# A linear-attention block with a gated feed-forward on one core: first tiles centred only, no self-waits on TensorE, half chunks joined, denominators sent through DRAM, folded weight in ten products

## The chip, the cores and the metric

The kernel runs on one core of a Trainium2 chip. The metric is the device time of one execution in microseconds (us). Executions of one kernel on the same chip are compared by the ratio of the means of their fast runs, with a 95% interval. A profile is one execution taken with the hardware profiler, and its span (first to last instruction) is 1.7 to 1.9 us shorter than the time of the same execution. A few executions of the kernel before lay over 1.5% above its fastest; they count as slow and are left out of the ratios.

## The reference, cut to what matters

```python
# x [1, 2048, 640], wqkv [640, 1920], wo [640, 640], w1 [640, 1728], w2 [1728, 640]; bf16; 32 heads of 20
xn  = layernorm(x)                              # no weight, no bias
q, k, v = split_heads(xn @ wqkv)
pq, pk  = phi(q), phi(k)                        # phi(t) = (t + 1 if t > 0 else exp(t)) + 1e-6
kv  = einsum("bhsd,bhse->bhde", pk, v)          # 20 x 20 per head
z   = einsum("bhsd->bhd", pk)
den = einsum("bhqd,bhd->bhq", pq, z) + 1e-6
s   = merge_heads(einsum("bhqd,bhde->bhqe", pq, kv) / den) @ wo
g   = silu(relu(xn @ w1) @ w2)
out = x + s * g
```

## The kernel before

Tokens are cut into 16 tiles of 128 (T) and four chunks of 512 (J); the model dimension into five blocks of 128 (C). The feed-forward width is 13 chunks of 128 and one half chunk of 64 rows. The kernel never forms V: it builds G = xn^T pk, and from it the small per-head matrices kv, and multiplies those with wo into one 640 x 640 weight for the query features (the folded weight). The order on TensorE is:

1. the opening: dummy matmuls that warm the clock, transposes, and the K products of the first four tiles;
2. the first-weight stage: Q and hidden (H) blocks of five matmuls 128x512, with the K tiles of the next chunk between them; near its end the denominators (den);
3. G: five blocks of 32 matmuls;
4. the second-weight stage and S: hidden times w2, its half chunks, the kv and folded-weight products in between, and per token tile an S product of ten matmuls, which VectorE multiplies by the gate and adds to x.

A small scheduler follows which engine last wrote and read each buffer, and puts the waits in. These are the parts that the change and the argument touch.

```python
# the scheduler: has engine E already seen `agent`?
return vc.get(agent[0], 0) >= agent[1] + 1
...
# loads, all on the SP queue: four x tiles, all of the K weights, all of the Q weights, then the rest
for t in range(4):
    x_load(t)
w_load(wqk[:, :, D:2 * D], A_wqkv[:, D:2 * D], ("wk",))
w_load(wqk[:, :, 0:D], A_wqkv[:, 0:D], ("wq",))
...
def LN_stats(t):          # VectorE: bn_stats twice, bn_aggr; GpSimd: + eps, then ** -0.5 -> rsy
    ...
def LN_norm(t):           # VectorE: (x - mean) * rsy
    last_norm[0] = sc.op("DVE", lambda eng: eng.tensor_scalar(
        out=xn[:, t, :], in0=xin[:, t % XR, :], scalar1=mv[:, t, 0:1], scalar2=rsy[:, t:t + 1],
        op0=ALU.subtract, op1=ALU.mult), R=[("xin", t % XR), ("mv", t), ("rsy", t)], W=[("xn", t)])
...
def z_add():              # GpSimd: adds one tile's pk to the running sum z
    t = zpend.pop(0)
    sc.op("POOL", lambda eng: eng.tensor_tensor(out=zacc[:, :], in0=zacc[:, :], in1=pk[:, t, :], op=ALU.add),
          R=[("zacc",), ("pk", t)], W=[("zacc",)])
...
# second weight: issued on SP as soon as the last H group has been read
for a in range(2):
    c0, c1 = (0, 7) if a == 0 else (7, NF)
    dma("SP", lambda eng, c0=c0, c1=c1: eng.dma_start(
        w2_sb[:, c0:c1, :], B_w2[P * c0:P * c1, :].rearrange("(c p) n -> p c n", p=P)),
        W=[("w2", a)], extra=[lastW1])
...
def expand(m):            # spreads 1/den from 32 heads over 128 features with four matmuls into PSUM
    fns = [(lambda eng, i=i: eng.matmul(ps[4 + i], lhsT=EmQ[H * i:H * (i + 1), m, :], rhs=rden[H * i:H * (i + 1), :],
                                        start=True, stop=True)) for i in range(J)]
    ...                   # and VectorE multiplies the query features by it
for k in range(C):
    lastG = G_block(k, gb[k % 2])
    expand(k)
...
def U(p, hook=None):      # two token tiles times w2: 26 matmuls, 26 more, then four half-chunk matmuls
    ...
```

Of the kernel before, what the change touches and what calls it, by code (L numbers as in the profile page):

```python
# [20 lines left out]
class Sched:  # L21
# [19 lines left out]
    def _known(self, E, agent):  # L41
        vc = self.vc[E]
        if agent[0] == "D":
            return vc.get(agent, False)
        return vc.get(agent[0], 0) >= agent[1] + 1
# [58 lines left out]
    def _update_res(self, agent, R, W):  # L104
# [8 lines left out]
        for key in W:  # L113
            st = self.res.get(key)
            if st is None:
                st = self.res[key] = _Res()
            else:
                assert st.w is None or st.nread > 0 or key in Rset or key in self.allow_unread, (
                    "unread overwrite of %r by %r (prev writer %r)" % (key, agent, st.w))
            st.w = agent  # L120
            st.r = {}
            st.nread = 0
# [89 lines left out]
def bass_recurrent_scan__linear_attn_block__dense_activation_relu__prompt_kernel(  # L212
# [23 lines left out]
    XR = 8  # L236

# [3 lines left out]
    h_lo = [(P * c) // DH for c in range(C)]  # L241
    h_hi = [-(-(P * (c + 1)) // DH) for c in range(C)]

    def cs_of_m(m):
        return [c for c in range(C) if DH * h_lo[c] < P * (m + 1) and DH * h_hi[c] > P * m]

    bf = dt.bfloat16
    f32 = dt.float32

# [12 lines left out]
    kvp = reg3[:, 0:C * D].rearrange("p (c n) -> p c n", c=C)  # L262
    outb = reg3[:, C * D:(C + NOUT) * D].rearrange("p (a n) -> p a n", a=NOUT)
    tmpo = reg3[:, (C + NOUT) * D:(C + 2 * NOUT) * D].rearrange("p (a n) -> p a n", a=NOUT)
# [18 lines left out]
    wo_sb = reg7[:, 0:C * D].rearrange("p (c n) -> p c n", c=C)  # L283
# [3 lines left out]
    ek = nc.alloc_sbuf_tensor("ek", [P, NEK, 2, D], bf)  # L287
    er = nc.alloc_sbuf_tensor("er", [P, NER, 2, 512], bf)
    ident = nc.alloc_sbuf_tensor("ident", [P, P], bf)
    EmQ = nc.alloc_sbuf_tensor("EmQ", [P, C, P], bf)  # L290
    mh = nc.alloc_sbuf_tensor("mh", [P, C, H], f32)
    zmat = nc.alloc_sbuf_tensor("zmat", [P, C, H], bf)
    zacc = nc.alloc_sbuf_tensor("zacc", [P, D], f32)
    zhl = nc.alloc_sbuf_tensor("zhl", [P, 2, D], bf)
    ones = nc.alloc_sbuf_tensor("ones", [P, 1], bf)
    mhalf = nc.alloc_sbuf_tensor("mhalf", [P, 1], f32)
    denS = nc.alloc_sbuf_tensor("denS", [P, 512], f32)
    rden = nc.alloc_sbuf_tensor("rden", [P, 512], bf)
    stats = nc.alloc_sbuf_tensor("stats", [P, T, 2, 6], f32)
    mv = nc.alloc_sbuf_tensor("mv", [P, T, 2], f32)  # L300
    rsv = nc.alloc_sbuf_tensor("rsv", [P, T], f32)
    rsy = nc.alloc_sbuf_tensor("rsy", [P, T], f32)

# [7 lines left out]
    NDS = 90  # L311
# [15 lines left out]

    def x_load(t):
        sl = t % XR
        dma("SP", lambda eng: eng.dma_start(xin[:, sl, :], x2[tok(t), :]), W=[("xin", sl)])  # L330

    def w_load(dst, src, key, extra=()):
        dma("SP", lambda eng: eng.dma_start(dst, src.rearrange("(c p) n -> p c n", p=P)), W=[key], extra=extra)

    for t in range(4):
        x_load(t)
    w_load(wqk[:, :, D:2 * D], A_wqkv[:, D:2 * D], ("wk",))
    w_load(wqk[:, :, 0:D], A_wqkv[:, 0:D], ("wq",))
    for t in range(4, XR):
        x_load(t)  # L340
    F1 = 7 * P
    w_load(w1_sb[:, :, 0:F1], B_w1[:, 0:F1], ("w1", 0))
    w_load(w1_sb[:, :, F1:FF], B_w1[:, F1:FF], ("w1", 1))


    sc.op("POOL", lambda eng: eng.memset(ident[:], 0.0), W=[("ident",)])
# [6 lines left out]
    NWARM = 42  # L353
    sc.group("PE", [(lambda eng: eng.matmul(ps[7][:, 0:P], lhsT=ident[:], rhs=ident[:], start=True, stop=True))
                    for _ in range(NWARM)], R=[("ident",)], W=[("ps", 7)])
    sc.allow_unread.add(("ps", 7))

    def build_consts():
        em = EmQ[0:H, :, :].rearrange("p c n -> p (c n)")
        sc.op("POOL", lambda eng: eng.memset(em, 1.0), W=[("Em",)])  # L360
        sc.op("POOL", lambda eng: eng.affine_select(out=em, in_=em, compare_op=ALU.is_ge, fill=0.0,
                                                    base=0, pattern=[[1, D]], channel_multiplier=-DH),
              R=[("Em",)], W=[("Em",)])
        sc.op("POOL", lambda eng: eng.affine_select(out=em, in_=em, compare_op=ALU.is_ge, fill=0.0,
                                                    base=DH - 1, pattern=[[-1, D]], channel_multiplier=DH),
              R=[("Em",)], W=[("Em",)])
        for qd in range(1, 4):
            dma("SP", lambda eng, qd=qd: eng.dma_start(EmQ[H * qd:H * (qd + 1), :, :], EmQ[0:H, :, :]),
                R=[("Em",)], W=[("Em4", qd)])
# [6 lines left out]
              R=[("mh",)], W=[("mh",)])  # L376


    def LN_stats(t):
        xv = xin[:, t % XR, :]  # L380
        for a in range(2):
            sc.op("DVE", lambda eng, a=a: eng.bn_stats(stats[:, t, a, :], xv[:, HN * a:HN * (a + 1)]),  # L382
                  R=[("xin", t % XR)], W=[("stats", t, a)])
# [5 lines left out]
                                                    op=ALU.pow), R=[("rsv", t), ("mhalf",)], W=[("rsy", t)])  # L389

# [8 lines left out]

    def transposes(t, b):  # L400
        psb = ps[b].bitcast(bf)
        sc.group("PE", [(lambda eng, c=c: eng.transpose(psb[:, P * c:P * (c + 1)], xn[:, t, P * c:P * (c + 1)], ident[:]))
                        for c in range(C)], R=[("xn", t), ("ident",)], W=[("ps", b)])

    def xnT_copy(t, b):
        psb = ps[b].bitcast(bf)
        sc.op("ACT", lambda eng: eng.activation(out=xnT[:, :, tok(t)],
                                                in_=psb[:, 0:C * P].rearrange("p (c q) -> p c q", c=C),
                                                func=ACTF.Copy), R=[("ps", b)], W=[("xnT", t)])
# [5 lines left out]
    def K_mm(t, b, halves=(0, 1)):  # L415
        fns = []
        for a in halves:
            for k in range(C):
                fns.append(lambda eng, a=a, k=k: eng.matmul(  # L419
                    ps[b + a][:, 0:HN], lhsT=xnT[:, k, tok(t)], rhs=wqk[:, k, D + HN * a:D + HN * (a + 1)],  # L420
                    start=(k == 0), stop=(k == C - 1)))
        sc.group("PE", fns, R=[("xnT", t), ("wk",)], W=[("ps", b + a) for a in halves])
# [7 lines left out]

    def K_exp(t, b):
        e_ = ek[:, t % NEK, 0, :]
        sc.op("ACT", lambda eng: eng.activation(out=e_.rearrange("p (a n) -> p a n", a=2), in_=ps2(b, HN), func=ACTF.Exp),  # L433
              R=[("ps", b), ("ps", b + 1)], W=[("ek_e", t % NEK)])

    def K_relu(t, b):
        r_ = ek[:, t % NEK, 1, :]
        sc.op("ACT", lambda eng: eng.activation(out=r_.rearrange("p (a n) -> p a n", a=2), in_=ps2(b, HN), func=ACTF.Relu),
              R=[("ps", b), ("ps", b + 1)], W=[("ek_r", t % NEK)])
# [11 lines left out]
    def K_ev(t, b):  # L451
        K_exp(t, b)
        K_relu(t, b)
        K_fin(t)

# [3 lines left out]
    def nextb():  # L459
        b = RB[ring[0] % len(RB)]  # L460
        ring[0] += 1
        return b

    qi = [0]

    def Q_block(j, f):
# [9 lines left out]
        if j == 0:  # L476
            sc.op("ACT", lambda eng: eng.activation(out=r_, in_=ps[b], func=ACTF.Relu), R=[("ps", b)], W=[("er_r", es)])
# [311 lines left out]
    for m in range(C):  # L789
        W_block(m)  # L790
# [39 lines left out]
```

## Time and profile before

| | before |
|---|---|
| time, median of 4 runs | 234.38 us (232.65 to 235.73) |
| span of the profile, mean clock | 233.1 us, 0.992 |
| first K matmul / end of the first four K tiles | 9.36 / 17.71 us |
| end of the first-weight stage (E) | 116.37 us |
| end of G | 140.2 us |
| last S matmul | 229.3 us |

(The prediction was made when three of the four runs were known, with a median of 233.63.)

To read a profile of such a kernel, one takes the busy shares and the slices first; they say which engine never rests. Here that is TensorE, so the rest of the time goes into the chain of work that ended last, read in order of time. The prediction below does this. Two more lines of the page of before are needed later. One is the group of the normalisations on VectorE (busy time, mean ns of one, then the engine's idle time before them), the other the memory traffic of the whole run.

### The profile page before, as it was taken

How to read it: one execution, taken by the hardware profiler on the slowest of the kernel's cores; microseconds unless marked ns; L12 is line 12 of the kernel's file. 1: busy time of each engine (PE TensorE's matmuls, PEld its weight loads, DVE VectorE, ACT ScalarE, POOL GpSimd, SP SyncE). 2: the span in 40 equal slices, each digit the busy share in tenths (PEclk: the TensorE clock that was granted, in tenths of full speed). 3: DMA queues.
4: the chain of work that ended last, by engine and by line, in shares of the span. 5: the costliest groups of instructions: out<-in, count | busy, mean ns of one | idle time of the engine just before them, and what ended most of it. 6: DMA issues, size and time to landing. Idle time of an engine off the chain costs nothing.

```text
span 233.1 us, 3514 instructions
## 1 busy us (share of the span) xinstructions
PE 223.4 (96%) x1461; PEld 134.7 (58%) x1471; DVE 104.8 (45%) x199; ACT 86.9 (37%) x141; POOL 47.5 (20%) x67
## 2 busy tenths in 40 slices
PE   7599999999999999999999999999999999999993
PEld 7464555544544555444466667666666667666662
DVE  4588941595527951681526446111230404041335
ACT  2289676655675666654521113322020202202020
POOL 4335923317623154420000004000000000000001
PEclk9979999999999999999999999999999999999999
DMA  5999620011400123000088007500101001010103
GB/s 166 376 399 182 138 106 3 0 30 42 61 6 0 28 59 28 0 0 3 0 272 265 0 0 262 191 0 3 58 0 59 28 28 59 0 56 3 56 0 113
DMA packets 20879, 17.95 MB, mean 77 GB/s; under 512 B 8864, under 2 KB 20864, under 8 KB 20864
## 3 DMA queue, kind: packets, MB, share of 16 engines
q1 hardware_dynamic: 20864, 17.74, 26.3%
q8 instruction: 11, 0.18, 0.3%
q14 instruction: 4, 0.03, 0.0%
HBM read 13.03 MB, written 2.62 MB: 67 GB/s over the span
## 4 chain that ended last, share of the span: by engine, by line
PE 87%; DVE 6%; DMA 4%; issue 1%; SPq 1%; ACT 0%; DVEq 0%
PE psT L715 25%; PE psT L491 21%; PE psT L665 10%; PE psT L419 9%; PE psT L743 9%; PE psT L468 7%; DMA reg<-in_A_wqkv_dram 3%; DVE pqT L485 2%; PE psT L692 2%; PE psT L725 1%; DVE er L483 1%; DMA reg<-reg 1%; PE psT L504 1%; SPq L330 1%; DVE stats L382 1%
## 5 line engine op out<-in xcount | busy, mean ns | idle before, releaser
L715 PE MATMUL psT<-reg,hT 128*128 128x320 bf16 x416 | 59.2, 299 | 0.4
L491 PE MATMUL psT<-reg 128*128 128x512 bf16 x252 | 56.8, 379 | 0.5 <-issue 0.2
L715 PEld LDWEIGHTS psT<-reg,hT 128*128 128x128 bf16 x416 | 40.0, 98 | 18.1 <-PE psT L715 2.7
L491 PEld LDWEIGHTS psT<-reg 128*128 128x128 bf16 x260 | 25.3, 98 | 29.2 <-issue 0.4
L495 ACT ACTIVATE hT<-psT 128x512 bf16<-128x512 f32 x52 | 31.1, 598 | 19.6 <-PE psT L491 19.5
L757 DVE TENSOR_TENSOR reg<-psT,reg 128x640 bf16<-128x640 f32 (+1 forms) x17 | 13.3, 784 | 55.6 <-PE psT L743 55.6
L732 ACT ACTIVATE reg<-psT 128x640 bf16<-128x640 f32 x16 | 10.4, 700 | 69.6 <-PE psT L725 69.6
L419 PE MATMUL psT<-reg 128*128 128x320 bf16 x160 | 25.8, 309 | 3.1 <-DMA reg<-in_A_wqkv_dram 2.6
L428 POOL TENSOR_TENSOR zacc<-zacc,reg 128x640 f32<-128x640 f32 x16 | 22.6, 1410 | 27.4 <-DVE reg L447 27.2
L743 PE MATMUL psT<-reg,pqT 128*128 128x320 bf16 x160 | 22.9, 299 | 0.0
L419 PEld LDWEIGHTS psT<-reg 128*128 128x128 bf16 x160 | 15.8, 101 | 11.9 <-issue 2.8
L665 PE MATMUL psT<-reg 128*128 128x320 bf16 x160 | 22.6, 299 | 0.0
L468 PE MATMUL psT<-reg 128*128 128x512 bf16 x98 | 21.8, 379 | 0.2 <-issue 0.2
L657 DVE TENSOR_TENSOR pqT<-pqT,psT 128x512 bf16<-128x512 bf16 x20 | 12.4, 682 | 16.6 <-PE psT L653 16.6
L743 PEld LDWEIGHTS psT<-reg,pqT 128*128 128x128 bf16 x160 | 15.1, 98 | 7.4 <-issue 1.9
L665 PEld LDWEIGHTS psT<-reg 128*128 128x128 bf16 x160 | 15.2, 98 | 7.0 <-issue 1.3
L760 POOL TENSOR_TENSOR reg<-reg 128x320 bf16<-128x320 bf16 x1 | 0.8, 789 | 87.0 <-DVE reg L757 87.0
L382 DVE BATCH_NORM_STATS2 stats<-reg 128x6 f32<-128x320 bf16 x32 | 14.0, 479 | 5.5 <-DMA reg<-in_A_x_dram 5.5
L468 PEld LDWEIGHTS psT<-reg 128*128 128x128 bf16 x100 | 9.7, 98 | 11.5 <-issue 0.4
L433 ACT ACTIVATE ek<-psT 128x640 bf16<-128x640 f32 x16 | 11.3, 704 | 10.6 <-PE psT L419 10.4
L445 DVE TENSOR_SCALAR ek<-ek 128x640 bf16<-128x640 bf16 x16 | 5.1, 320 | 21.6 <-ACT ek L433 21.4
L475 ACT ACTIVATE er<-psT 128x512 bf16<-128x512 f32 x20 | 12.0, 599 | 7.5 <-PE psT L468 4.7
(59 smaller groups left out, 151.8 us busy)
## 6 DMA issues: line engine op xcount, KB each, us to landing
reg<-in_A_x_dram SPq DMA_DIRECT2D x16, 160.0 KB, 6.6
reg<-in_A_x_dram SPq DMA_DIRECT2D x4, 640.0 KB, 6.9
out_dram<-reg SPq DMA_DIRECT2D x15, 160.0 KB, 1.8
reg<-in_B_w_dram SPq DMA_DIRECT2D x2, 1120.0 KB, 7.6
reg<-in_A_wqkv_dram SPq DMA_DIRECT2D x2, 800.0 KB, 7.4
reg<-in_B_w_dram SPq DMA_DIRECT2D x1, 1040.0 KB, 12.2
reg<-in_B_w_dram SPq DMA_DIRECT2D x1, 960.0 KB, 8.4
wv_sb<-in_A_wqkv_dram SPq DMA_DIRECT2D x1, 800.0 KB, 5.1
```

What stands on the lines that cost most here:

```text
L382: sc.op("DVE", lambda eng, a=a: eng.bn_stats(stats[:, t, a, :], xv[:, HN * a:HN * (a + 1)]), R=[("xin", t % XR)], W=[("stats", t, a)])
L419: fns.append(lambda eng, a=a, k=k: eng.matmul(ps[b + a][:, 0:HN], lhsT=xnT[:, k, tok(t)], rhs=wqk[:, k, D + HN * a:D + HN * (a + 1)], star ...
L428: sc.op("POOL", lambda eng: eng.tensor_tensor(out=zacc[:, :], in0=zacc[:, :], in1=pk[:, t, :], op=ALU.add), R=[("zacc",), ("pk", t)], W=[( ...
L468: sc.group("PE", [(lambda eng, k=k: eng.matmul(ps[b], lhsT=wqk[:, k, P * f:P * (f + 1)], rhs=xnT[:, k, schunk(j)], start=(k == 0), stop=(k ...
L475: sc.op("ACT", lambda eng: eng.activation(out=e_, in_=ps[b], func=ACTF.Exp), R=[("ps", b)], W=[("er_e", es)])
L491: a = sc.group("PE", [(lambda eng, k=k: eng.matmul(ps[b], lhsT=w1_sb[:, k, P * f:P * (f + 1)], rhs=xnT[:, k, schunk(j)], start=(k == 0), s ...
L495: sc.op("ACT", lambda eng: eng.activation(out=hT[:, f, schunk(j)], in_=ps[b], func=ACTF.Relu), R=[("ps", b)], W=[("hT", j, f)])
L657: sc.op("DVE", lambda eng, i=i: eng.tensor_tensor(out=pqT[:, m, schunk(i)], in0=pqT[:, m, schunk(i)], in1=ps[4 + i], op=ALU.mult), R=[("ps ...
L665: fns.append(lambda eng, t=t, a=a: eng.matmul(ps[b + a][:, 0:HN], lhsT=xn[:, t, P * k:P * (k + 1)], rhs=pk[:, t, HN * a:HN * (a + 1)], sta ...
L715: fns.append(lambda eng, u=u, t=t, f=f, n=n: eng.matmul(ps[bs[n] + u][:, 0:HN], lhsT=hT[:, f, tok(t)], rhs=w2_sb[:, f, HN * n:HN * (n + 1) ...
L743: sc.group("PE", [(lambda eng, c=c, a=a: eng.matmul(ps[b + a][:, 0:HN], lhsT=pqT[:, c, tok(t)], rhs=wf[:, c, HN * a:HN * (a + 1)], start=( ...
L757: sc.op("DVE", lambda eng: eng.tensor_tensor(out=tmpo[:, os_, lo:hi].rearrange(shp, a=na), in0=src, in1=g_sb[:, t, lo:hi].rearrange(shp, a ...
```

## The change

The intent is to take TensorE's hiccups away. The K products of the first four tiles run on x minus its mean, and the factor 1/sigma comes in later as a scale on ScalarE. TensorE no longer waits for its own earlier groups. The half chunks of two pairs are done in one group of eight. The spreading of 1/den leaves TensorE: the reciprocals are written to DRAM twenty-fold and read back in the layout that VectorE needs. The kv matrix is cut into six blocks of whole heads instead of five of 128 rows, so that each block of the folded weight needs two contractions instead of two or three: ten passes, 20 matmuls, where 26 were. Q blocks and S products are spread between other work. The diff cut to its core:

```diff
@@ scheduler @@
+        if E == "PE" and agent[0] == "PE":
+            return True
@@ loads @@
-    for t in range(4):
-        x_load(t)
-    w_load(wqk[:, :, D:2 * D], A_wqkv[:, D:2 * D], ("wk",))
-    w_load(wqk[:, :, 0:D], A_wqkv[:, 0:D], ("wq",))
+    x_load(0)
+    x_load(1)
+    w_load(wqk[:, 0:KA, D:2 * D], A_wqkv[0:KA * P, D:2 * D], ("wk", 0))      # KA = 3
+    x_load(2)
+    w_load(wqk[:, KA:C, D:2 * D], A_wqkv[KA * P:D, D:2 * D], ("wk", 1))
+    x_load(3)
...
@@ first tiles @@
+    def centre(t):                      # x - mean only; mean from ScalarE's accumulator
+            sc.op("DVE", lambda eng: eng.tensor_scalar(
+                out=xn[:, t, :], in0=xin[:, t, :], scalar1=msum[:, t, 1:2], scalar2=None,
+                op0=ALU.subtract), R=[("xin", t), ("msum", t, 1)], W=[("xn", t)])
+    def K_evac(t, b, func, slot, key):
+        scale = rsy[:, t:t + 1] if t < 4 else 1.0
...
@@ den(), right behind the reciprocal @@
+        for i in range(J):
+            src = rden[H * i:H * (i + 1), :].unsqueeze(1).to_broadcast([H, DH, 512])
+            dst = scr[:, schunk(i)].rearrange("(h e) s -> h e s", e=DH)
+            dma("SP", lambda eng, src=src, dst=dst: eng.dma_start(dst, src), R=[("rden",)], W=[("scr", i)])
+        for m in range(C):
...
+            dma("SP", lambda eng, m=m: eng.dma_start(Rr[m], scr[P * m:P * (m + 1), :]),
+                R=[("scr", i) for i in range(J)], W=[("Rr", m)], extra=ex)
@@ order of the z adds @@
-                if n >= 6 and zpend:
-                    z_add()
+            if n >= 3 and zpend and len(zpend) > (1 if j < J - 1 else 0):
+                z_add()
@@ G @@
     for k in range(C):
-        lastG = G_block(k, gb[k % 2])
-        expand(k)
+        lastG = G_block(k, (0, 2)[k % 2])
@@ second-weight stage @@
-    def U(p, hook=None):
...
+    def U_sub(p, u, n):                 # 13 matmuls into one bank
+    def U_halves(p):                    # eight half-chunk matmuls for two pairs
...
+        for i in (0, 1, 2, 3):          # behind the kv blocks
+            divide(i)                   # VectorE: query features times the read-back reciprocals
```

Not shown: the loads of the Q weights and of the second part of the first weight move from SP's queue to ScalarE's. The loads of w2 stay where they were in the text, which is now behind the writes and reads of the round trip on the same queue.

## The prediction

> **What bounds the kernel now.** I read the page from the top: busy shares, the slices, then the chain that ended last.
>
> ```profile
> PE 223.4 (96%) x1461; PEld 134.7 (58%) x1471; DVE 104.8 (45%) x199; ACT 86.9 (37%) x141; POOL 47.5 (20%) x67
> PE   7599999999999999999999999999999999999993
> PEclk9979999999999999999999999999999999999999
> PE 87%; DVE 6%; DMA 4%; issue 1%; SPq 1%; ACT 0%; DVEq 0%
> ```
>
> TensorE is busy in every slice but the first two and the last, and carries 87% of the chain. No other engine passes 45%. So only four things can pay: fewer matmuls, fewer hiccups between them, an earlier first one, a shorter tail. From the chain in order of time: the first K matmul starts at 9.36 us, the K tiles of the first chunk end at 17.71, the first-weight stage (call its end E) at 116.37, G at 140.2, and the last S matmul near 229.3; 3.8 us of tail follow. Busy matmuls are at their rate: in the chain 20 of 128x512 take 4.32 us (216 ns each), 26 of 128x320 take 3.54 (136 ns). The groups' 379 and 299 ns are pipelined durations and must not be multiplied by the count.
>
> The hiccups, first in the chain (start, length, piece), then in the windows (busy per engine, clock, DMA share, GB/s):
>
> ```profile
> 153.01 3.54 PE psT L715 x26
> 156.56 0.05 issue
> 156.61 3.71 PE psT L715 x26
> 160.31 0.38 PE psT L725 x4
> 160.69 2.82 PE psT L743 x20
> ```
> ```profile
> 9.00:10.00 1.00, 0.64 (x5) 0.51 (x6) 0.45 (x1) 0.00 (x0) 0.13 (x1) 1.00 1.06 370
> 11.00:12.00 1.00, 1.00 (x8) 0.83 (x7) 0.03 (x1) 0.70 (x2) 0.00 (x0) 0.50 1.05 381
> 12.00:13.00 1.00, 1.00 (x6) 0.57 (x4) 0.96 (x3) 1.00 (x3) 0.00 (x0) 0.50 1.05 398
> 13.00:14.00 1.00, 1.00 (x9) 0.77 (x8) 0.76 (x4) 0.49 (x2) 0.73 (x2) 0.50 1.05 401
> ```
>
> The second half of each pair in the second-weight stage (L715) loses 0.05 + 0.17 us, because its group waits for TensorE's own count: seven times, 1.5 us. The four half-chunk matmuls take 0.38 us where two full ones would take 0.27. TensorE stood idle from 6.8 to 9.36 us, then ran at half clock from about 10.85 to 14.05 us, which cost 1.6 us.
>
> **What the Trainium skill says.**
> (1) "TensorE: Matmul & The Clock Gate", Part 1: an idle window of about 3.4 us puts the array back to half clock, and it takes about as long to leave it. The trace agrees: 2.6 us of idleness were followed by 3.2 us at 0.50.
> (2) "TensorEngine Tiling (Array Packing)", Key Properties: changing the tiling mode drains TensorE. The trace agrees: the weight loads of the 64-row groups, and of what follows them, sit idle 0.26 us each.
> (3) "SBUF — State Buffer", Door 1: a transfer on 32 or 64 partitions reaches only half of the 16 ports; 189 GB/s for 32 partitions at 1 MiB. The trace leans that way: while the two 64-partition loads passed, the rate fell though the share stayed full:
> ```profile
> 119.50:120.00 0.50, 0.50 (x6) 0.35 (x5) 0.00 (x0) 0.00 (x0) 0.00 (x0) 1.00 1.05 389
> 124.00:124.50 0.50, 0.50 (x6) 0.35 (x5) 0.00 (x0) 0.00 (x0) 0.00 (x0) 1.00 1.14 251
> ```
> (4) "DMA: Bandwidth & Descriptors", Rules for kernel authors: a DMA that reads what another wrote must wait for that one's semaphore. The diff does so, on the SP queue. No run yet shows that wait.
>
> **The change part by part.**
> *Start.* K weights come in two parts right behind two x tiles: 0.8 MB precede the first K matmul instead of 1.44. Moved bytes in the windows reach 0.73 MB by 5 us and 1.03 by 6; landing followed the last byte by 1 to 2 us. So the first K can go at about 6.7 us. Centring skips the aggregate and the two POOL steps (0.21 + 0.23 + 0.57 us), but K still waits for weights. The rest of wk (1.28 MB down the queue) lands near 8.5, x3 near 9; then TensorE has 4.7 us of K and transposes, ScalarE puts two exponentials' worth (2 x 0.70) and a DMA issue ahead of the last copy, and a half-clock spell is still likely. I put the end of the K tiles at 15.0 (14 to 16) instead of 17.71: 2.7 us saved.
> *First-weight stage.* The same 72 blocks of five (77.8 us), 12 K tiles (16.4) and 3.8 us of halves, z and den: 98 us. Before took 98.66 with 0.5 us waiting for a transpose. Spread Q blocks ease VectorE (1.48 us per Q and LN work against 2.2 us of TensorE per pair of blocks). Four more transposes by DMA may cost the first chunk 0.5. E = 15.0 + 98.8 = 113.8.
> *G.* Expand goes: five times 0.33 us plus the drains round it. G alone is 160 x 0.1363 = 21.8 us instead of 23.8: 2.0 saved.
> *Second-weight stage and S.* 416 x 0.1363 = 56.7; halves in four groups of eight at about 0.65: 2.6 instead of 3.0; S 22.1 instead of 22.6 (fewer drains ahead of it); folded weight 20 x 0.1363 = 2.7 instead of 3.6; kv 30 short ones, 1.65 instead of 1.56. Sum 85.8 instead of 89.1 (the self-waits are the rest).
> *Tail.* VectorE now does both last adds (0.3 to 0.5 each) behind a Silu of 0.70; near 3.8 us as before.
> Sum without new waits: 113.8 + 21.8 + 85.8 + 3.8 = 225.2 us of span, 3.4% less.
>
> *What it adds.* The reciprocals go to DRAM twenty-fold (32 heads x 20 x 2048 x 2 bytes = 2.62 MB) and come back as 2.62 MB; VectorE's 20 multiplies move off PSUM (682 ns) and are hidden. But SP issues in program order. Before, it issued the second weight at E:
>
> ```profile
> 116.40 1.00 SPq L636 DMA_DIRECT2D reg<-in_B_w_dram  x2
> 117.45 1.19 SPq L640 DMA_DIRECT2D reg<-in_B_w_dram  x2
> 118.68 0.59 SPq L333 DMA_DIRECT2D reg<-in_A_wo_dram  x1
> ```
>
> After, four writes, the wait for them, and five reads stand in front of the second weight, and every group of the second-weight stage needs all of that weight. The time line, counted from E: den ends at E - 3.4 (three H blocks follow it); the sum (0.69) and reciprocal give rden at E + 0.8.
>
> ```profile
> L583 DVE RECIPROCAL rden<-denS 128x512 bf16<-128x512 f32 x1 | 3.4, 3353 | 0.0
> ```
>
> Data flows from E + 2.4; 2.62 MB at 360 GB/s take 7.3 us, at about 200 (point 3: each write has 32 partitions as source) 12.5. The last landing is 0.7 us later: E + 10.5 or E + 15.8. The reads take 1.8 us to full rate and 6.7 us at 390 GB/s: E + 19 or E + 24.3. The second weight, 2.08 MB behind them, takes 5.4 + 0.7: E + 25.1 or E + 30.4. G ends at E + 21.8. So TensorE stands **3.3 us or 8.6 us** before the second-weight stage, and the gap may bring back the half clock, for up to 1.6 us more.
>
> **The rivals.**
> (a) *Fast writes.* At over 400 GB/s the wait is 2 us or less and the clock holds: about 227. For it: SBUF sources have no HBM read. Against it: no transfer in this trace stays above 410.
> (b) *Port-bound writes.* 8.6 + 1.6 us: about 235.5, all the gain lost. For it: the dip to 251 GB/s and the skill's table. Against it: two short transfers are thin evidence, and they are writes into SBUF, not reads.
> (c) *The round trip is hidden anyway.* 225.5. It would need 7.3 MB in 19 us with no latencies; I give it 5%.
> (d) *VectorE or ScalarE bounds the opening or the Q-heavy second chunk.* VectorE has some 25 us of work in 30 there; that would cost 1 to 2 us.
>
> **Range and chances.** The middle between the 3.3 us wait (225.2 + 0.5 from span to measured time + 3.3 + 1 for the clock = 230) and the port-bound case (235.5), with some weight on (a), gives **231.0 us**. The base is uncertain by 1.5 us. Range 226.0 to 237.0. Faster by 2% needs less than 229.0: 0.33. Within 2%: 0.60. Slower: 0.07.
>
> **What would show it right or wrong.** The first K matmul near 6.7 us and the end of the K tiles near 15; no self-wait gaps in L715's successor; G blocks of 4.36 us without breaks; the writes' landing time against 7.3 or 12.5 us; a wait of the first second-weight matmul for a DMA from in_B_w, 3 to 9 us long, with a clock below 1.0 behind it. I am wrong if the second weight lands before G ends, if the opening is held by ScalarE's queue beyond 16 us, or if S waits for the divides.

## More of the kernel before

```profile
L394 DVE TENSOR_SCALAR reg<-reg,mv,rsy 128x640 bf16<-128x640 bf16 x16 | 8.0, 501 | 6.7 <-POOL rsy L388 6.7
HBM read 13.03 MB, written 2.62 MB: 67 GB/s over the span
```

A normalisation takes 501 ns in the mean, and the DMA engines are idle for most of the run.

## The result, and the profile after

The changed kernel took **240.85 us** (median of 4 runs, 240.14 to 241.82) against 234.38 (4 runs, 232.65 to 235.73). All ratios here are the mean time of one kernel's fast runs over the mean of the other's of the same rounds, so not quite the ratio of these medians. It is 1.0332, with a 95% interval of 1.0256 to 1.0408: slower by 3.3%, and outside the predicted range.

The page of the changed kernel, in the parts that the prediction showed of before: busy shares, TensorE by 40 slices (6 us each) in tenths, its granted clock, the traffic, and the chain by engine.

```profile
PE 219.2 (91%) x1425; PEld 134.0 (56%) x1436; DVE 112.5 (47%) x211; ACT 87.8 (37%) x144; POOL 45.0 (19%) x69
PE   6899969999999989999999912999999999999994
PEclk9999999999999999999999995799999999999998
HBM read 15.81 MB, written 5.24 MB: 88 GB/s over the span
PE 64%; DMA 14%; DVE 13%; SPq 3%; POOL 2%; issue 2%; ACT 1%; DVEq 0%
```

TensorE does 4 us less work than before (219.2 against 223.4), so the removals are real. But it has two holes it did not have: one near 30 us (a 6 among nines) and one near 140 us (a 1 and a 2), and in the second slice of the latter and the one behind it the clock is 0.5 and 0.7. In the chain, DMA has gone from 4% to 14% and VectorE from 6% to 13%. The list of waits of TensorE (total us, times, longest) names the holes:

```profile
PE psT L811 <- DMA reg<-in_B_w_dram: 9.5, 1, 9.5
PE psT L471 <- DMA reg<-reg: 2.9, 3, 2.3
PE psT L471 <- ACT hT L550: 0.7, 1, 0.7
```

The first is the second weight, the second the transposes that the K tiles read. (The kernel before had 0.5 us of the latter and none of the former.)

**The hole at 140 us.** Here is the chain in order of time (start, length, piece), from the reciprocal to the first second-weight matmuls:

```profile
114.74 3.36 DVE regE L660
118.12 0.69 SPq L666
...
121.77 10.71 DMA scr<-regE
132.49 0.34 SPq L672
...
135.31 13.15 DMA reg<-in_B_w_dram
148.46 0.09 issue
148.55 3.62 PE psT L811 x13
152.18 1.90 PE psT L774 x30
```

VectorE makes the reciprocals, SP issues four writes to DRAM, and the last of them lands at 132.5 us. Only then does SP issue the reads, and only behind the reads the second weight, which lands at 148.46. G had ended at 139.05. The SP queue's own timeline (start, length, line, what, count) has the order:

```profile
118.12 5.83 SPq L666 DMA_DIRECT2D scr<-regE  x4
132.49 1.76 SPq L672 DMA_DIRECT2D regE<-scr  x4
134.30 0.47 SPq L672 DMA_DIRECT2D regX<-scr  x1
134.82 1.85 SPq L742 DMA_DIRECT2D reg<-in_B_w_dram  x2
```

Between 123.95 and 132.49 us the queue does nothing but wait for its own writes. Before, the second weight was issued at 116.4. And the first 13 matmuls behind the hole take 3.62 us; at full rate they take 13 x 0.1363 = 1.77, so 1.85 us went to half clock.

How fast the writes went is in the windows (us; after the engines' busy times, the last three columns are clock, DMA share and GB/s):

```profile
122.00:124.00 2.00, 2.00 (x17) 1.43 (x15) 0.00 (x0) 0.40 (x1) 0.00 (x0) 1.00 0.94 213
124.00:126.00 2.00, 2.00 (x17) 1.43 (x16) 0.00 (x0) 0.00 (x0) 0.00 (x0) 1.00 0.95 208
126.00:128.00 2.00, 2.00 (x17) 1.44 (x15) 0.00 (x0) 0.70 (x1) 0.00 (x0) 1.00 0.97 243
136.00:138.00 2.00, 2.00 (x17) 1.44 (x15) 0.00 (x0) 0.00 (x0) 0.00 (x0) 1.00 1.00 371
```

The DMA engines report a share of 0.94 to 1.00 in all four, but the writes, whose source is 32 partitions, move 208 to 213 GB/s, and the reads that follow 371. The step to 243 falls where, by the order of the writes, one from the lower half of the partitions and one from the upper are under way at once.

**The hole at 30 us.** The chain runs here through VectorE and GpSimd. In the timeline both engines start within 0.06 us of each other (start, length, engine, line, what; the bracket is what the first waited for):

```profile
30.25 2.87 POOL L482 TENSOR_TENSOR zacc<-zacc,reg 128x640 f32<-128x640 f32 x2
30.31 2.99 DVE L413 TENSOR_SCALAR reg<-reg,mv,rsy 128x640 bf16<-128x640 bf16 x2 [0.46 <-POOL rsy L402]
```

Two adds into z on GpSimd, two normalisations on VectorE, and each normalisation takes 1.50 us. So do nine of the sixteen in this profile (the other seven take 0.43 to 0.45 us); before it was one of sixteen. That raises the mean from 501 to 1051 ns:

```profile
L413 DVE TENSOR_SCALAR reg<-reg,mv,rsy 128x640 bf16<-128x640 bf16 x16 | 16.5, 1051 | 3.3 <-POOL rsy L402 3.3
```

The pair starts together because both were held by the same thing: GpSimd computes rsy and turns to its next instruction, the add; VectorE waits for that rsy. The Trainium skill, "SBUF — State Buffer", section "Who interferes with whom", says that VectorE and GpSimd share one pair of SBUF ports, that a tensor_scalar can enter the modes that need it, and that whoever issues first holds the pair while the other blocks. The durations here agree in kind: 1.50 us beside an add, 0.44 alone.

The stages of the two kernels, in us of their profiles:

| | before | after | after - before |
|---|---|---|---|
| end of the first four K tiles | 17.71 | 15.2 | -2.5 |
| first-weight stage (its length) | 98.66 | 101.9 | +3.2 |
| G (its length) | 23.83 | 21.9 | -1.9 |
| wait for the second weight | 0 | 9.5 | +9.5 |
| second-weight stage and S, with 1.85 of half clock | 89.1 | 87.75 | -1.3 |
| tail | 3.8 | 3.5 | -0.3 |
| span | 233.1 | 239.8 | +6.7 |

### The profile page after: what moved, and what is told of

It is laid out like the page before. It is cut to its first block, busy times and chain, and to the rows that moved or that the text cites. A ratio compares the mean times of both kernels' runs of the same rounds, so it can differ in the third digit from the quotient of the medians.

```text
span 239.8 us, 3474 instructions
## 1 busy us (share of the span) xinstructions
PE 219.2 (91%) x1425; PEld 134.0 (56%) x1436; DVE 112.5 (47%) x211; ACT 87.8 (37%) x144; POOL 45.0 (19%) x69
## 3 DMA queue, kind: packets, MB, share of 16 engines
q10 hardware_dynamic: 1312, 1.88, 2.4%
## 4 chain that ended last, share of the span: by engine, by line
PE 64%; DMA 14%; DVE 13%; SPq 3%; POOL 2%; issue 2%; ACT 1%; DVEq 0%
PE psT L811 25%; PE psT L546 13%; PE psT L850 8%; PE psT L524 8%; PE psT L471 6%; DMA reg<-in_B_w_dram 5%; DMA scr<-regE 4%; DVE reg L413 3%; DVE stats L394 3%; DMA reg<-reg 2%; DMA reg<-in_A_wqkv_dram 2%; POOL rsy L402 2%; DVE pqT L534 2%; SPq L666 1%; DVE regE L660 1%
## 5 line engine op out<-in xcount | busy, mean ns | idle before, releaser
L811 PE MATMUL psT<-reg,hT 128*128 128x320 bf16 x416 | 62.2, 304 | 9.5 <-DMA reg<-in_B_w_dram 9.5
L546 PE MATMUL psT<-reg 128*128 128x512 bf16 x191 | 45.5, 379 | 0.3 <-issue 0.2
L546 PEld LDWEIGHTS psT<-reg 128*128 128x128 bf16 x195 | 19.0, 98 | 22.1 <-ACT hTl L567 0.4
L524 PE MATMUL psT<-reg 128*128 128x512 bf16 x95 | 23.8, 379 | 0.3
L839 ACT ACTIVATE reg<-psT 128x640 bf16<-128x640 f32 x12 | 8.2, 702 | 43.1 <-PE psT L811 23.6
L759 PE MATMUL psT<-reg 128*128 128x320 bf16 x160 | 21.9, 299 | 0.0
L471 PE MATMUL psT<-reg 128*128 128x320 bf16 x120 | 18.3, 299 | 3.6 <-DMA reg<-reg 2.9
L488 ACT ACTIVATE regE<-psT 128x640 bf16<-128x640 f32 x24 | 15.6, 701 | 13.4 <-PE psT L471 13.4
L759 PEld LDWEIGHTS psT<-reg 128*128 128x128 bf16 x160 | 15.7, 98 | 6.2
L532 DVE TENSOR_SCALAR regE<-psT 128x512 bf16<-128x512 f32 x20 | 13.6, 680 | 11.3 <-ACT regE L531 11.3
L413 DVE TENSOR_SCALAR reg<-reg,mv,rsy 128x640 bf16<-128x640 bf16 x16 | 16.5, 1051 | 3.3 <-POOL rsy L402 3.3
L471 PEld LDWEIGHTS psT<-reg 128*128 128x128 bf16 x120 | 11.3, 97 | 11.2 <-ACT hT L550 3.0
L839 ACT ACTIVATE reg<-psT,rsy 128x640 bf16<-128x640 f32 x4 | 3.2, 794 | 35.3 <-PE psT L829 30.1
L524 PEld LDWEIGHTS psT<-reg 128*128 128x128 bf16 x100 | 9.7, 98 | 11.4
L534 DVE SCALAR_TENSOR_TENSOR pqT<-regE 128x512 bf16<-128x512 bf16 x20 | 15.3, 766 | 0.7
## 6 DMA issues: line engine op xcount, KB each, us to landing
reg<-in_A_x_dram SPq DMA_DIRECT2D x4, 640.0 KB, 10.6
```

The costliest lines, as they stand in the source:

```text
L413: last_norm[0] = sc.op("DVE", lambda eng: eng.tensor_scalar(out=xn[:, t, :], in0=xin[:, t % XR, :], scalar1=mv[:, t, 0:1], scalar2=rsy[:, ...
L471: fns.append(lambda eng, a=a, k=k, lhs=lhs: eng.matmul(ps[b + a][:, 0:HN], lhsT=lhs[:, k, tok(t)], rhs=wqk[:, k, D + HN * a:D + HN * (a + 1)],
L488: sc.op("ACT", lambda eng: eng.activation(out=o_.rearrange("p (a n) -> p a n", a=2), in_=ps2(b, HN), func=func, scale=scale), R=[("ps", b) ...
L524: sc.group("PE", [(lambda eng, k=k: eng.matmul(ps[b], lhsT=wqk[:, k, P * f:P * (f + 1)], rhs=xnT[:, k, schunk(j)], start=(k == 0), stop=(k ...
L532: sc.op("DVE", lambda eng: eng.tensor_scalar(out=r_, in0=ps[b], scalar1=0.0, scalar2=1e-6, op0=ALU.max, op1=ALU.add), R=[("ps", b), ("er_e ...
L534: sc.op("DVE", lambda eng: eng.scalar_tensor_tensor(out=pqT[:, f, schunk(j)], in0=e_, scalar=1.0, in1=r_, op0=ALU.min, op1=ALU.add), R=[(" ...
```

## The experiments

Eleven kernels ran; all of them gave correct results. Each edit is against the changed kernel unless said otherwise, and each ratio is against the kernel before.

| run | what | median us | ratio (95% interval) |
|---|---|---|---|
| e1_w2_first | w2 issued ahead of the round trip | 231.03 | 0.9823 (0.9765 to 0.9880) |
| e2_w2_first_divlate | the same, divides later | 230.74 | 0.9779 (0.9726 to 0.9833) |
| e3_expand_kept | no round trip, spreading on TensorE | 232.05 | 0.9870 (0.9811 to 0.9929) |
| e11_source128 | the writes from 128 partitions | 237.60 | 1.0138 (1.0082 to 1.0194) |
| e6_dram_spread | twenty-fold copy inside DRAM | 245.52 | one look |
| e5_keep_warm | dummy matmuls in the hole | 239.53 | 1.0272 (1.0198 to 1.0345) |
| e4_zadd_later | no z add in the first chunk | 246.01 | 1.0446 (1.0408 to 1.0484) |
| e9_zadd_behind_norm | e2, z add behind the normalisation | 227.09 | 0.9720 (0.9653 to 0.9787) |
| e7_wk_whole | K weights in one piece | 244.41 | one look |
| e8_before_noself | before, with no self-waits | 233.39 | 0.9978 (0.9916 to 1.0040) |
| e10_best | e9, other banks, more warming | 226.79 | 0.9668 (0.9623 to 0.9713) |

Two theories for the hole at 140 us went into the first runs. ORDER: the weight is late only because it stands behind the round trip on its queue. TRAFFIC: 5.2 MB more make it late wherever it stands.

### e1: the second weight ahead of the round trip

```diff
@@ den() @@
         sc.op("DVE", frec, R=[("denS",)], W=[("rden",)])
+
+    def round_trip():
         for i in range(J):
             ...                                     # the four writes and the five reads
@@ loads of the second weight @@
     for u in range(2):
         dma("SP", lambda eng, u=u: eng.dma_start(w2l[64 * u:64 * (u + 1), :], B_w2[NF * P:FF, :]),
             W=[("w2l", u)], extra=[lastW1])
+    round_trip()
```

> The changed kernel with one difference: the second weight (and its half chunk) is issued on SP ahead of the four writes and five reads of the round trip. Theory ORDER (the 9.5 us wait and the 1.9 us of half clock behind it exist only because the second weight stands behind the round trip on SP): the wait for in_B_w falls from 9.5 us to under 1 us, 13 matmuls of the first group take 1.8 us instead of 3.6, clock 1.0 throughout, and 240.85 falls by up to 11.4 us to 229.5. Part may come back: the round trip now ends some 6 us later, the divides stand ahead of the folded weight's casts on VectorE and the output weight lands later, so up to 3 us of waiting there, 232.5. Rival TRAFFIC (the bytes themselves are too many, and whatever goes last is waited for): the wait moves whole to the folded weight or S and the time stays above 237.

It took 231.03 us (230.42 to 233.15, 4 runs): 5.1 points of the ratio better than the changed kernel, about 12 us. The wait for the second weight is gone from its list of waits; what TensorE still waits for at this place is the copy of the last G block. Two of the waits that remain, and the chain behind E:

```profile
PE psT L471 <- DMA reg<-reg: 2.8, 3, 2.3
PE psT L815 <- ACT reg L768: 0.8, 1, 0.8
```
```profile
117.91 21.75 PE psT L763 x160
...
140.44 1.94 PE psT L815 x13
```

G runs in one piece of 21.75 us, the second stage starts 0.8 us after it, and the first 13 matmuls take 1.94 us, not 3.62. The same 5.2 MB move, behind the weight, and cost nothing that one sees. ORDER is confirmed and TRAFFIC refuted. The saving of 9.5 + 1.85 - 0.8 = 10.6 us in the chain lies close to the 12 us of the timing; the rest was not followed up.

### e2: the divides later as well

```diff
-        for i in (0, 1, 2, 3):                       # in the hook behind the kv blocks
-            divide(i)
+    def divides(): ...                               # the same loop
-        (1, 2): [lambda: W_block(4, 0)],
+        (1, 2): [lambda: W_block(4, 0), divides],
```

> As e1, and the twenty divides stand behind the folded weight's casts in VectorE's order instead of ahead of them. If in e1 the folded weight waited for casts that queue behind the divides (and those behind the read-back), it gains those 2 to 3 us over e1: about 229.5 to 230.5. If e1 had no such wait, the same as e1.

It took 230.74 us (228.77 to 231.32), ratio 0.9779; the interval overlaps with that of e1. Behind the first-weight stage its list of waits is the same as that of e1. Its profile is 2.8 us shorter, but the difference lies in the opening (first K matmul at 5.92 us, six K matmuls in 0.98 us instead of 1.76), which the edit doesn't touch. In e1 the read-back reciprocals held nothing up, then: this edit changed nothing.

### e3: the spreading stays on TensorE

The round trip and the divides were taken out, and the four matmuls with their constants put back behind each G block, as before.

```diff
     for k in range(C):
         lastG = G_block(k, (0, 2)[k % 2])
+        expand(k)
```

> The changed kernel with one part undone: the reciprocals are expanded by TensorE between the G blocks as before, no DRAM round trip. Theory ORDER: the 11.4 us go (wait 0, clock 1.0) and 1.9 us of expand and drains come back in G (blocks of 4.45 plus 0.33 us): 240.85 - 11.4 + 1.9 = 231.3. If the round trip were hidden and the loss had another cause, the time would stay at 240 or rise by 2.

It took 232.05 us (231.62 to 234.39), ratio 0.987. This is the changed kernel without the one part that hurt, and it beats before, though by less than 2%. Between the G blocks its chain has the four matmuls at 0.33 us:

```profile
116.62 4.35 PE psT L763 x32
120.97 0.33 PE psT L751 x4
121.30 4.45 PE psT L763 x32
```

Five such groups, and four G blocks longer by 0.10 to 0.12, come to about 2.1 us, as the prediction had put the gain of the round trip (2.0). In the timing e3 stands 0.9% above e2, and the intervals overlap. So by the traces the round trip takes about 2 us out of G if its order is right, which the timing does not resolve, and if it is not, the whole is some 11 us worse than without it (4.6 points of the ratio).

### e11 and e6: why the writes were slow

SOURCE: 32 source partitions halve the rate of the writes. WRITE: writes of this kind, in pieces of 1 KB to DRAM, are slow whatever they come from. Run e11 keeps the order of the changed kernel and lays the buffer in DRAM out so that each of the four writes has all 128 partitions as source, with a quarter of the copies.

```diff
-    scr = nc.dram_tensor("scr", [D, S], bf, kind="Internal").ap()
+    scr = nc.dram_tensor("scr", [P, DH, 512], bf, kind="Internal").ap()
...
-            src = rden[H * i:H * (i + 1), :].unsqueeze(1).to_broadcast([H, DH, 512])
-            dst = scr[:, schunk(i)].rearrange("(h e) s -> h e s", e=DH)
+            src = rden[:, :].unsqueeze(1).to_broadcast([P, DH // J, 512])
+            dst = scr[:, DH // J * i:DH // J * (i + 1), :]
```

> The changed kernel, order of issue untouched, but each of the four writes of 640 KB takes all 128 partitions as source (the copy in DRAM is laid out by partition, still in 1 KB pieces; the read-back gathers 1 KB pieces instead of 4 KB). Theory SOURCE (32 partitions as source held the writes to 210 GB/s): writes at 350 GB/s or more, the last landing 9 us after rden instead of 14.4, the second weight lands some 5 us sooner and the wait for it falls from 9.5 us to 3 to 5; time 5 to 6 us below the changed kernel, ratio about 1.01. Rival WRITE (1 KB pieces into DRAM at 210 GB/s whatever the source): landing after 14 us again, wait 9 us or more, ratio 1.03 to 1.04.

It took 237.60 us (236.92 to 238.97), ratio 1.0138. Its windows of the writes, and its wait:

```profile
122.00:124.00 2.00, 2.00 (x17) 1.43 (x16) 0.00 (x0) 0.70 (x1) 0.00 (x0) 1.00 1.03 335
124.00:126.00 2.00, 2.00 (x17) 1.43 (x16) 0.00 (x0) 0.00 (x0) 0.00 (x0) 1.00 1.03 346
```
```profile
PE psT L813 <- DMA reg<-in_B_w_dram: 5.8, 1, 5.8
```

The same bytes in pieces of the same size go at 335 to 346 GB/s instead of 208 to 213. The edit also changes where the pieces lie in DRAM, but that is not what held the writes: in e6, below, pieces go to the old places at up to 343 GB/s. SOURCE is confirmed. The last write lands 9.1 us after the first was issued (14.4 before), as expected. The wait falls from 9.5 to 5.8 us, by less than the expected 3 to 5 us would have it, since from there to the landing of the second weight it takes 17.5 us instead of 16.0; the reads now gather pieces of 1 KB, but what took the 1.5 us was not tested. The ratio falls by 1.9 points (some 4.5 us). The first 13 matmuls still take 3.62 us: the shorter wait costs the same half clock.

Run e6 wrote the reciprocals once to DRAM (four times 32 KB) and made the twenty copies from DRAM to DRAM.

```diff
+            dma("SP", lambda eng, i=i: eng.dma_start(scr2[:, schunk(i)], rden[H * i:H * (i + 1), :]),
+                R=[("rden",)], W=[("scr2", i)])
...
+            src = scr2[:, schunk(i)].unsqueeze(1).to_broadcast([H, DH, 512])
```

> The changed kernel, but the reciprocals go to DRAM once (four writes of 32 KB), and the twenty-fold copy is made from DRAM to DRAM with the same 2.62 MB and the same 1 KB pieces. Theory SOURCE (the four writes took 13 us because each reads 32 partitions): the copies move at over 300 GB/s, some 8 us, and with about 2.5 us for the extra step the last lands some 12.5 to 13 us after rden instead of 14.4; the wait for in_B_w shrinks from 9.5 to about 8. Rival WRITE (1 KB pieces into DRAM are slow whatever the source): the copies take 13 us again and the wait grows to about 12.

In its one look it took 245.52 us, with a wait of 13.5 us where 8 were expected: a miss. The copies took 16 us, from 120.05 to 136.5. Their rate was uneven: at the best

```profile
126.00:128.00 2.00, 2.00 (x17) 1.46 (x15) 0.00 (x0) 0.70 (x1) 0.00 (x0) 1.00 1.13 343
```

and about 100 GB/s at the end. The run changes two things, the source and the kind of copy, so by itself it decides nothing between the two theories; it shows that this way is no better, and that the old places in DRAM take more than 213 GB/s.

### e5: TensorE kept busy in the hole

The question was whether the slow start of the second stage is half clock. Between G and that stage 42 matmuls of 128x512 were put whose result nobody reads.

```diff
+    NKEEP = 42
+    sc.group("PE", [(lambda eng: eng.matmul(ps[7], lhsT=ident[:], rhs=hT[:, 0, 0:512], start=True, stop=True))
+                    for _ in range(NKEEP)], R=[("ident",), ("hT", 0, 0)], W=[("ps", 7)])
```

> The changed kernel with 42 dummy matmuls of 512 columns (42 x 216 ns = 9.1 us) between G and the second-weight stage, where TensorE only waited. Results are thrown away. Theory CLOCK (after the wait the array runs at half clock, and that costs 1.9 us in the profiled run and more in executions with a lower mean clock): the first 13 matmuls take 1.8 us instead of 3.6, mean clock 0.99 instead of 0.976 or lower, time 2 to 4 us below the changed kernel, ratio to before about 1.02 instead of 1.033 to 1.04. Rival: the slow first group is something else (fresh weights, a full queue), then nothing changes or the dummies push the stage back.

In its chain the dummies fill the hole, and the first 13 matmuls are back at their rate:

```profile
139.27 9.01 PE psT L888 x41
148.29 1.88 PE psT L811 x13
```

The mean granted clock was 1.000 in every run of this kernel, after 0.976. Its span is 2.3 us shorter. In the trace this is clear; in the timing (239.53 us, 239.22 to 241.79; ratio 1.0272 against 1.0332) the intervals overlap.

### e4: no z add in the first chunk (the remedy failed)

Theory PORT: the adds on GpSimd stretch VectorE's normalisations, and the transposes behind them come late. The rival is that full DMA queues make the transposes late; another is that the K tiles stand too early in the new order, so that the transposes would be late without any collision. In e4 the adds of the first chunk are put off to the second.

```diff
-            if n >= 3 and zpend and len(zpend) > (1 if j < J - 1 else 0):
+            if j > 0 and n >= 3 and zpend and len(zpend) > (1 if j < J - 1 else 0):
```

> The changed kernel with one difference: GpSimd adds no K tile to the z sum during the first chunk; those adds run from the second chunk on. Theory PORT (VectorE's normalisations took 1.5 us instead of 0.4 in that chunk because the z adds on GpSimd hold what they share, so the transposes for K tiles 4 to 7 start late): the normalisations fall to 0.4 to 0.5 us there, TensorE's waits for transposes fall from 2.9 to under 1 us, the time falls by 2 to 2.5 us to about 238.5. Rival DMA (the transposes are late because the DMA queues are full): normalisations may speed up, but the waits stay and so does 240.8.

The time was a miss: 246.01 us (242.5 to 246.12, 6 runs), slower than the changed kernel. In the first chunk it did what was expected: the normalisations took 0.43 to 0.44 us there, the wait for transposes fell from 2.6 to 0.4 us, and the last K tile of the chunk started at 32.45 instead of 35.08. So neither rival holds there. But the adds, now four at a time, met VectorE in the second chunk instead:

```profile
52.14 6.36 POOL L482 TENSOR_TENSOR zacc<-zacc,reg 128x640 f32<-128x640 f32 x4
65.39 1.52 PE L471 MATMUL psT<-reg 128*128 128x320 bf16 x10 [2.88 <-DMA reg<-reg]
```
```profile
PE psT L471 <- DMA reg<-reg: 5.3, 4, 2.9
```

Four adds in a row, and one K tile that waits 2.88 us; 5.3 us of such waits in all, and E at 119.4. The normalisations of that chunk are no longer than in the changed kernel (1.52 us). What grew is other work of VectorE beside the adds: the two operations that finish a K tile took 1.51 and 1.60 us instead of 0.32 and 0.49, and two normalisations in turn stand 8.7 us apart instead of 5.9. The mean clock was also lower in the timed executions (0.963 to 0.977, against 0.986 in the profile), and their spans longer (241.5 to 244.4 us against 240.8); why is not shown. The mechanism was right, and the remedy only moved the collision.

### e9: the z add behind the normalisation

On top of e2, an add into z waits for the last normalisation, and from the second chunk on no add is put where a tile's statistics are computed.

```diff
     def z_add():
         sc.op("POOL", ..., R=[("zacc",), ("pk", t)], W=[("zacc",)]
+              , extra=[last_norm[0]])
...
-            if n >= 3 and zpend and len(zpend) > (1 if j < J - 1 else 0):
+            if n >= 3 and (j == 0 or n not in lnat[j]) and zpend and len(zpend) > (1 if j < J - 1 else 0):
```

> e2 (second weight first, divides late) with the z adds on GpSimd made to wait for the normalisation that was issued last, so that the two do not start together. Theory PORT: normalisations take 0.4 to 0.6 us on average instead of 1.05, TensorE's waits for transposes fall from 2.8 to under 1 us, 1.5 to 2.5 us under e2: ratio about 0.969 instead of 0.978. Rival: the collision moves to VectorE's next instruction and K still waits, same as e2.

It took 227.09 us (225.97 to 228.39), ratio 0.972. The query of this one line, for the changed kernel and then for e9 (first figures: shortest, median, longest in ns; then first and last start in us):

```profile
L413 DVE TENSOR_SCALAR reg<-reg,mv,rsy x16: 434/1512/1552, 17.2 to 86.1; 128x640 bf16<-128x640 bf16 x16
```
```profile
L413 DVE TENSOR_SCALAR reg<-reg,mv,rsy x16: 440/442/447, 17.0 to 83.2; 128x640 bf16<-128x640 bf16 x16
PE psT L471 <- DMA reg<-reg: 0.3, 1, 0.3
```

All sixteen normalisations now take 440 to 447 ns, 2.6 us of waits for transposes are gone (2.9 to 0.3), the wait of 0.7 us for ScalarE at a K tile is gone with them, and E falls from 117.1 to 113.2. These 3.3 us and 0.2 from the opening are most of the 3.9. The rival was right in half: some collisions do move to VectorE's next instruction (one that finishes a K tile takes 1.57 us at 24.58 us, behind an add at 24.39), but K hardly waits any more. PORT is confirmed, since the K tiles stand in the same places of the order. That the shared thing is the ports is the skill's account; the runs show the collision. The gain rests on the traces: against e2, on which it builds, the ratio moves by 0.6 points (some 1.4 us, where 1.5 to 2.5 were expected), and the intervals overlap. The opening of e2's profile happened to be 2.1 us shorter; its first-weight stage takes 102.1 us, that of e9 98.2.

### e7: the K weights in one piece

```diff
-    w_load(wqk[:, 0:KA, D:2 * D], A_wqkv[0:KA * P, D:2 * D], ("wk", 0))
+    w_load(wqk[:, :, D:2 * D], A_wqkv[:, D:2 * D], ("wk", 0))
     x_load(2)
-    w_load(wqk[:, KA:C, D:2 * D], A_wqkv[KA * P:D, D:2 * D], ("wk", 1))
```

> The changed kernel with the K weight loaded in one piece of 800 KB instead of two. Theory: the first K matmul waits for weights, not for the centred tile, so it starts about 1.5 us later (8.3 instead of 6.8 us), and the centred tile's copy is ready at 5.6 us as before. The end of the K tiles moves by less than that, since their second half waited for the second piece before. Rival: the opening hangs on the tiles' own chain, then the first K matmul stays within 0.5 us of 6.8.

244.41 us, span 242.7. The centred copy was ready as early as in the changed kernel, and the first K matmul waited:

```profile
8.49 1.76 PE L470 MATMUL psT<-reg,regX 128*128 128x320 bf16 x6 [3.39 <-DMA reg<-in_A_wqkv_dram]
```

It starts at 8.49 us instead of 6.84, and the delay grows on the way (the last K tile of the first chunk starts at 37.54 us instead of 35.08, and the wait for the second weight was 10.4 us). So the splitting of the load is what lets the opening go earlier; the centring by itself is hidden behind that load.

### e8: the kernel before, with the self-waits taken out

The scheduler's edit alone, in the kernel before (with the check on unread buffers loosened to match).

```diff
+        if E == "PE" and agent[0] == "PE":
+            return True
```

> The kernel before with one part of the change alone: TensorE does not wait on its own count. By the prediction's sum seven gaps of 0.05 us and the slow restart of 0.17 us behind each go: 1.5 us, ratio 0.9935, and in the chain every 26 matmuls of the second-weight stage take 3.54 us with no piece of 0.05 before them. Rival: the weight loads there wait for something else, ratio 1.000.

It took 233.39 us (232.2 to 234.6), ratio 0.9978 (0.9916 to 1.0040): not resolved. In the chain a pair of the second-weight stage is one piece,

```profile
164.51 7.06 PE psT L718 x52
```

where before had 3.54 + 0.05 + 3.71 = 7.30 us. From the start of G to the last S matmul of the chain it needs 109.87 us, before 111.50: 1.63 us saved, as the prediction had (1.5). In this profile the opening was slower (the first K matmul waited 3.4 us for its weights, against 2.6, and the first five took 1.49 us instead of 0.84), so G began 1.2 us later, which hides most of that.

### e10: more of the same

On top of e9: the two PSUM banks of G swapped, so that the second stage needn't wait for the last copy, and 16 more dummy matmuls in the opening.

```diff
-        lastG = G_block(k, (0, 2)[k % 2])
+        lastG = G_block(k, (2, 0)[k % 2])
-    NWARM = 28
+    NWARM = 30
+    sc.group("PE", [... matmul(ps[7][:, 0:P], lhsT=zero[:], rhs=zero[:] ...) for _ in range(14)], ...)
```

> e9 with two small mends: G's last block uses the other pair of PSUM banks, so that the second-weight stage does not wait for its copy (0.8 us in e9), and 16 dummy matmuls more keep TensorE going in the opening, so that the first six K matmuls run at full clock (0.98 us, as in e2's profile, instead of 1.76). By the sum 1.6 us under e9: ratio to before about 0.965. If the opening is bound by the loads after those six, only the 0.8 us.

It took 226.79 us (225.86 to 227.83, 6 runs), ratio 0.9668: 3.3% faster than before, and not to be told from e9. Both edits work where they are (six K matmuls in 0.97 us instead of 1.76; the wait of 0.8 us behind G is gone), but two new waits take the gain:

```profile
PE psT L471 <- DMA reg<-reg: 1.4, 2, 0.8
PE psT L780 <- DVE reg L783: 1.0, 1, 1.0
```

The K tiles arrive earlier than their transposes. And the kv products wait for VectorE, which waits for a 3.30 us clearing of a buffer on GpSimd that can't start before G has ended.

The recorded clock does not explain the first of the two gains. Between 7 and 9 us it reads 1.00 in e9, where the six matmuls take 1.76 us, as in e10, where they take 0.97. So a recorded 1.00 does not prove full rate; the durations have to be read as well.

## Why the prediction was wrong

- **What bounds the kernel** was right. Every hole on TensorE went straight into the time.
- **Start: right.** First K matmul at 6.84 us (predicted 6.7), K tiles done at 15.2 (15.0). e7 shows that the weights set it, as said.
- **First-weight stage: wrong, by 3.3 us.** The step "The same 72 blocks of five (77.8 us), 12 K tiles (16.4) and 3.8 us of halves, z and den: 98 us", with 0.5 for transposes and a rounding up to 98.8, took each engine's work at its rate alone. It lacked the collision of GpSimd's adds with the normalisations, which the new order made frequent (nine of sixteen instead of one). E came at 117.1 instead of 113.8. With that cause removed (e9) E is 113.2, so the rest of the sum was sound. Rival (d), VectorE in the second chunk at "1 to 2 us", named the engine but not the reason.
- **G, second stage, S, tail: right.** 21.9 us (21.8), 85.9 without the half clock (85.8), 3.5 (3.8).
- **The round trip: mechanism right, branch weighed wrongly.** The prediction worked out two cases: landing at E + 10.5 with a wait of 3.3 us, or at E + 15.8 with 8.6 us and up to 1.6 of half clock. The second came true: E + 15.4, 9.5 us and 1.85 us. It was rival (b), "Port-bound writes". The step that failed is the last one: "The middle between the 3.3 us wait [...] and the port-bound case (235.5), with some weight on (a), gives 231.0 us". The ground for doubt, that the thin evidence was "writes into SBUF, not reads", did not hold: e11 shows that it is the partitions that count in this direction too.
- **From span to time: 1.2 us short.** The prediction took 0.5 us, the median of three runs (233.63) less the span of one profile (233.1). Each execution has 1.7 to 1.9. The 235.5 of the port-bound case left this step out altogether: 225.2 + 8.6 + 1.6 = 235.4 is a span.
- **The errors add.** The case with the 3.3 us wait was put at 230. Onto it come 6.2 us of longer wait (9.5), 3.3 of first-weight stage, 0.9 of half clock (1.85 instead of 1) and these 1.2: 241.6. The profiled execution took 241.52. The collision alone would not have left the range (231.0 + 3.3 = 234.3). The port-bound case would have: as predicted it is 235.4 + 1.7 = 237.1 in time, and with the wait and the half clock as measured 238.3, above the 237.0 at which the range ends.
- **Two readings were loose.** 2.62 MB at "about 200" GB/s take 13.1 us; 12.5 belong to 210, which is near what was measured. And the trace of before agrees with the skill's clock window only in part: TensorE stood idle for 2.6 us, less than the 3.4 named, and the clock fell at 10.7 us, 1.3 us after it had started again.

## What to carry to other kernels

A queue issues in the order of the program, so a load that the critical engine needs soon must not stand behind a chain of transfers that wait for each other: moving the loads of the second weight by a few lines was worth 5% here. When the same event releases two engines that share something, they can collide again and again (here nine times in sixteen, before once); make one wait for the other's short instruction. And a long wait of TensorE can be paid a second time in clock, here 1.85 us for 9.5 and for 5.8 us alike. In both cases the recorded clock fell about 4 us after TensorE had stopped. No run tells how short a wait is safe: behind 0.8 us the first 13 matmuls took 1.94 us (e1).

## What the Trainium skill lacked or had wrong

- "SBUF — State Buffer", section "Door 1", does not say of its rates by number of partitions whether they were taken loading or storing. For stores to DRAM the loss on 32 partitions holds here: 208 to 213 GB/s from 32 partitions, 335 to 346 from 128 (e11), and 243 where stores from both halves overlapped.
- "SBUF — State Buffer", section "Who interferes with whom", is right that the two engines collide, and the runs do not contradict it that the loser blocks until the other has finished: a normalisation that starts 0.06 us after an add and one that starts 0.27 us after it (46.32 us, beside an add from 46.05 to 47.66) both end 0.1 to 0.2 us behind the add. That is less than the 0.44 us that it takes alone, so some of its time passes while it is blocked, or GpSimd's times in the trace, which are rough, are off.
- The same section doesn't say how such collisions become systematic: two instructions on two engines that can start at one event. Median of the normalisations 1512 ns with, 442 ns without (e9).
- "TensorE: Matmul & The Clock Gate", Part 1, agrees with the runs: half clock behind 9.5 and 5.8 us of waiting, none when dummies fill it (e5: clock 1.000, 1.88 us for 13 matmuls instead of 3.62). Why executions of one kernel differ in their mean clock (e4: 0.963 to 0.986) was not examined here.
- No page has the rate of a copy from DRAM to DRAM in pieces of 1 KB: 2.62 MB took 16 us here, with a best window of 343 GB/s and some 100 at the end (e6).
